# Turning the second part's inputs with VectorE blocks and short DMA runs instead of TensorE transposes, in a long-convolution + gated-MLP kernel

## The chip, the cores and the metric

The kernel runs on one core of one Trainium2 chip. The metric is the device time of the program in microseconds (us); before the change it is 3759.47 us, the median of three runs (3757.68 to 3761.73). The engines are named as in the profile: PE (TensorE matmuls), PEld (TensorE's weight loads, which overlap PE), DVE (VectorE), ACT (ScalarE), POOL (GpSimd) and SP (SyncE, whose queue issues every DMA of this kernel).

## The reference

Everything is float32 in and out.

```python
# first part: x, v are (4, 12480, 128); pos_emb (12480, 64), w1 (64, 64), w2 (64, 128)
h_filt = (np.maximum(pos_emb @ w1, 0.0) @ w2) * np.exp(-0.01 * pos)[:, None]
u = x * v
y = irfft(rfft(u, 2 * S, axis=1) * rfft(h_filt, 2 * S, axis=0))[:, :S, :]   # causal long convolution
z = x * y
# second part: z as (49920, 128); w_in (128, 2048), w_out (2048, 128)
h = z @ w_in
out = (h * np.cos(h)) @ w_out
```

## The kernel before, in words

**First part, the convolution.** Each of the 4 batches is seen as 104 rows (n1, `R`) by 120 columns (n2, `N2`). A forward transform in two stages (`f1`, `f2`), a product with the filter's transform and an inverse transform in two stages (`i1`, `i2`) are all done as matmuls. The last stage, `i2_units`, makes one *group* at a time: 4 values of n2 (`G`), that is 104 rows by 4 x 128 numbers, 30 groups a batch (`NG`), 120 in all. A group is two halves of 4 matmuls (`i2_mm`, L504) with the twiddle table `tm` as weights, and then `i2_out`: VectorE multiplies the PSUM bank by the input x (`xs`) into `zs` (L511), and SP stores the 104 x 512 tile to the DRAM scratch `zd` (L517). While a batch is in `i2`, SP also loads `tm` (312 KB) and `xs` for the next group and, for the next batch, `xt` and `vt`, whose product fills `slots`. In batch 0 most `tm` tables are made on the spot by ACT, DVE and POOL (`make_group`) and stored for the later batches.

**Second part, the MLP.** The 12480 rows of groups (each of 4 tokens) are cut into 98 *blocks* (`NALL`): block 0 is the first group (104 rows), the rest are of 128 rows, the last of 88. A block therefore has up to 512 tokens. Its input must stand with the 128 features on the partitions and the tokens along the free side (`at`). Before the change, `moe_load(n)` (L727) loads 128 rows of `zd` as `zb` (128 x 4 x 128), and `moe_turn(n)` makes four TensorE transposes of 128 x 128 into one PSUM bank (the `transpose` helper, L126) and one ACT copy to `at` (L737). Block 0 skips the DRAM trip: its `zs` is turned directly.

Each block is 16 *steps* (`NFC`). A step is one matmul of 128 x 512 into `ph` (L743), `a` on ACT (L746), the rounding `k` on DVE (L749), the difference `f` on POOL (L752), the sine `cs` on ACT (L757), the product `gt` on DVE (L759), and four steps later (`LAG`) a matmul that adds to `acc` (L768). At the block's end ACT copies `acc` out (L774), four more transposes turn it back, ACT copies them to `ob` (L783) and SP stores it (L794). That is 1568 steps. A 128 x 512 float32 matmul is two passes on TensorE.

**The order of the work.** The program is written in a fixed order (manual schedule), and each engine runs its own instructions in that order. The main loop walks the 1568 steps; after each step it advances the convolution generator `conv` by what the step is owed (`owed`; a unit of `conv` says what it costs in steps). So the first part of batches 1 to 3 runs between the steps of the second part. `load(n)` first advances `conv` until the rows of block n are made. Before the change, `load(n + 2)` is called at step 12 of block n, and `moe_turn(n + 1)` at step 3 of block n. From about 345 us on both parts run together, until the last group at about 2949 us; after that only steps remain.

The SP queue, too, is in order: a DMA whose wait is not met holds all that are behind it. The framework gives DMAs eight completion semaphores in turn, so that a DMA also waits until the one eight places ahead of it has landed.

Tile pools that matter: `zs`, `tm` and `xs` have 2 buffers each in batches 0 to 2 (`tm` and `xs` 3 in the last), `zb` and `at` 2, and the `ph` banks are 4, shared by the steps and the transposes.

Of the kernel before, what the change touches and what calls it, by code (L numbers as in the profile page):

```python
# [9 lines left out]
F32 = mybir.dt.float32  # L10
U32 = mybir.dt.uint32
AF = mybir.ActivationFunctionType
ALU = mybir.AluOpType
# [3 lines left out]
P = 128  # L17
BANK = 512
# [12 lines left out]
def kernel(  # L31
# [46 lines left out]
    nc = tc.nc  # L78

    B, S, D = x.shape  # L80
# [3 lines left out]
    R = S // N2  # L84
# [14 lines left out]
    NFC = DFF // P  # L99
    G = BANK // D  # L100
    UA = 2
    NG = N2 // G
    NROWS = B * NG * R
    NALL = 1 + math.ceil((NROWS - R) / P)
    assert G == 2 * UA and H % UA == 0 and N2 % G == 0
    LAG = 4
    WCOL = 256

    dram = ctx.enter_context(tc.tile_pool(name="dram", bufs=1, space=DRAM))
    hd = dram.tile([N1 // 2, N2, 2, CB, 4], F32, name="hd")  # L110
    zd = dram.tile([NROWS, G, D], F32, name="zd")
    wd = dram.tile([N1 // 2, KE, 2, N2], F32, name="wd")
    td = dram.tile([N2 // G, N1, G, 2, R], F32, name="td")
    wind = dram.tile([D, DFF], F32, name="wind")
# [9 lines left out]
    def transpose(dst, src, ident):  # L124
        n = src.shape[0]
        nc.tensor.transpose(dst, src, ident[0:n, 0:n])  # L126


    def float32_parts(pool, raw):
        lo, hi = raw[:, :, 0], raw[:, :, 1]  # L130

        power = pool.tile([P, WCOL], U32, name="power", bufs=2)
        nc.vector.tensor_scalar(out=power[:, :], in0=hi, scalar1=20, scalar2=0x7FF,
# [5 lines left out]

        sig = pool.tile([P, WCOL], U32, name="sig", bufs=2)  # L140
        nc.vector.tensor_scalar(out=sig[:, :], in0=hi, scalar1=0xFFFFF, scalar2=0x100000,
                                op0=ALU.bitwise_and, op1=ALU.bitwise_or)
        high = sig[:, :].bitcast(F32)
        nc.scalar.activation(high, sig[:, :], AF.Copy, scale=2.0 ** -20)
        low = pool.tile([P, WCOL], F32, name="low", bufs=1)
        nc.scalar.activation(low[:, :], lo, AF.Copy, scale=2.0 ** -52)
# [3 lines left out]
    def float32_join(dst, raw, power, high):  # L150
# [6 lines left out]
        if dst.space == DRAM:  # L157
# [3 lines left out]
    out_words = moe_w_out.bitcast(U32).rearrange("(c p) (q w) -> p c q w", p=P, w=2)  # L161
    in_pieces = [(slice(c, c + WCOL), in_words[:, c:c + WCOL, :])
                 for c in range(0, DFF, WCOL)]
    out_pieces = [(slice(c, c + WCOL // D), out_words[:, c:c + WCOL // D, :, :])
                  for c in range(0, NFC, WCOL // D)]
# [110 lines left out]
    def last_tables(pool):  # L276
        rows = pool.tile([N1, 4, R], F32, name="rows")

        tw_t = pool.tile([N1, 2, N2], F32, name="tw_t")
        return rows, tw_t  # L280
# [226 lines left out]
    def i2_out(pool, ps, xs, b, g):  # L507
        if b == 0:
            yield
        zs = pool.tile([R, 2, UA, D], F32, name="zs")  # L510
        nc.vector.tensor_tensor(  # L511
            zs[:, :, :, :].rearrange("p h n d -> p (h n d)"), ps[0:R, :],
            xs[:, :, :].rearrange("p h n -> p (h n)"), op=ALU.mult)
        z = zs[:, :, :, :].rearrange("p h n d -> p (h n) d")
        row = (b * NG + g) * R
        if row > 0:
            nc.sync.dma_start(zd[row:row + R, :, :], z)  # L517
        else:
            zbs[0] = z
        made[0] += 1  # L520
        yield

    rows_psum = []
    made = [0]
    zbs = {}

# [187 lines left out]
    ats, accs = {}, {}  # L716

    def first_row(n):
        return min(R + (n - 1) * P, NROWS) if n else 0

    def rows_of(n):
        return first_row(n + 1) - first_row(n)

    def moe_load(pool, n):
        m, row = rows_of(n), first_row(n)
        zb = pool.tile([P, G, D], F32, name="zb", bufs=2)
        nc.sync.dma_start(zb[0:m, :, :], zd[row:row + m, :, :])  # L727
        zbs[n] = zb

    def moe_turn(pool, n):  # L730
        m = rows_of(n)
        zb = zbs.pop(n)
        pt = ps_h.tile([P, BANK], F32, name="ph")
        for i in range(G):
            transpose(pt[:, i * m:(i + 1) * m], zb[0:m, i, :], ident)
        at = pool.tile([D, BANK], F32, name="at")
        nc.scalar.copy(out=at[:, 0:G * m], in_=pt[:, 0:G * m])  # L737
        ats[n] = at

    def moe_up(pool, n, c):  # L740
        m = G * rows_of(n)
        ph = ps_h.tile([P, BANK], F32, name="ph")
        nc.tensor.matmul(ph[:, 0:m], w_in_sb[:, c * P:(c + 1) * P], ats[n][:, 0:m],  # L743
                         start=True, stop=True)
        a = pool.tile([P, BANK], F32, name="a", bufs=3)
        nc.scalar.activation(a[:, 0:m], ph[:, 0:m], AF.Identity,  # L746
                             bias=quarter[:, 0:1], scale=INV_TWO_PI)
        k = pool.tile([P, BANK], F32, name="k")
        nc.vector.tensor_scalar(out=k[:, 0:m], in0=a[:, 0:m], scalar1=ROUND,  # L749
                                scalar2=ROUND, op0=ALU.add, op1=ALU.subtract)  # L750
        f = pool.tile([P, BANK], F32, name="f")
        nc.gpsimd.tensor_tensor(f[:, 0:m], a[:, 0:m], k[:, 0:m], op=ALU.subtract)  # L752
        return ph, f, m

    def moe_act(pool, ph, f, m):
        cs = pool.tile([P, BANK], F32, name="cs")
        nc.scalar.activation(cs[:, 0:m], f[:, 0:m], AF.Sin, scale=TWO_PI)  # L757
        gt = pool.tile([P, BANK], F32, name="gt", bufs=4)
        nc.vector.tensor_tensor(gt[:, 0:m], ph[:, 0:m], cs[:, 0:m], op=ALU.mult)  # L759
        return gt  # L760

    def moe_down(n, c, gt):
        if c == 0:

            accs[n] = bank() if made[0] == B * NG and n % 2 else \
                ps_acc.tile([P, BANK], F32, name="acc")
        m = G * rows_of(n)
        nc.tensor.matmul(accs[n][:, 0:m], w_out_sb[:, c, :], gt[:, 0:m],  # L768
                         start=(c == 0), stop=(c == NFC - 1))

    def moe_evict(pool, n):
        m = G * rows_of(n)
        ot = pool.tile([D, BANK], F32, name="ot", bufs=1)
        nc.scalar.copy(out=ot[:, 0:m], in_=accs.pop(n)[:, 0:m])  # L774
        return ot

    def moe_back(pool, n, ot):
        m = rows_of(n)
        pt = ps_h.tile([P, BANK], F32, name="ph")
        for i in range(G):  # L780
            transpose(pt[0:m, i * D:(i + 1) * D], ot[:, i * m:(i + 1) * m], ident)
        ob = pool.tile([P, 2, UA * D], F32, name="ob", bufs=1)
        nc.scalar.copy(out=ob[0:m, :, :].rearrange("p h n -> p (h n)"), in_=pt[0:m, :])  # L783
        return ob
# [15 lines left out]
    with tc.manual_schedule():  # L800
        with tc.tile_pool(name="psum", bufs=8, space=PSUM) as psum, \
                ExitStack() as first:
            def bank():
                return psum.tile([P, BANK], F32, name="ps")
# [11 lines left out]
            with tc.tile_pool(name="layers", bufs=1, side="right") as pool:  # L816
# [14 lines left out]
                ident = pool.tile([P, P], F32, name="ident")  # L831
# [65 lines left out]
            rows, tw_t = last_tables(wpool)  # L897
            for kept, here in ((rowsd, rows), (twd, tw_t)):
                nc.sync.dma_start(here[:, :, :], kept[:, :, :])
            ident = wpool.tile([P, P], F32, name="ident")  # L900
# [17 lines left out]
        nc.scalar.copy(out=table, in_=rows[:, :, :])  # L918
        rows_psum.append(table)
        mpool = ctx.enter_context(tc.tile_pool(name="moe", bufs=2))  # L920

        def bank():
            return ps_c[0].tile([P, BANK], F32, name="cv")
# [15 lines left out]
        def load(n):  # L939
            while made[0] * R < first_row(n + 1):  # L940
                next(conv)
            moe_load(mpool, n)

        while made[0] == 0:
            next(conv)
        moe_turn(mpool, 0)
        steps = [(n, c) for n in range(NALL) for c in range(NFC)]
        hidden, gates, ots, obs = {}, {}, {}, {}
        for i in range(len(steps) + LAG):
            if i < len(steps):  # L950
                n, c = steps[i]
                if n == 0 and c == NFC // 2:
                    load(1)
                if c == NFC - 4 and n + 2 < NALL:
                    load(n + 2)
                hidden[i] = moe_up(mpool, n, c)
            if i >= LAG:
                pn, pc = steps[i - LAG]
                moe_down(pn, pc, gates.pop(i - LAG))
                if pc == NFC - 1:  # L960
                    ots[pn] = moe_evict(mpool, pn)
            if 0 <= i - 1 < len(steps):
                gates[i - 1] = moe_act(mpool, *hidden.pop(i - 1))
            if i < len(steps):

                if c == (LAG - 1 if n else NFC - 2) and n + 1 < NALL:
                    moe_turn(mpool, n + 1)
                if c == NFC // 2 and n - 1 in ots:
                    obs[n - 1] = moe_back(mpool, n - 1, ots.pop(n - 1))
                if c == NFC // 2 + 2 and n - 1 in obs:  # L970
                    moe_store(n - 1, obs.pop(n - 1))
            owed += 1.0
            while owed > 0.0:
                owed -= next(conv, owed)
# [30 lines left out]
```

## Time and profile before

| | |
|---|---|
| device time, median of 3 runs | 3759.47 us (3757.68 to 3761.73) |
| the profiled execution, first to last instruction | 3758.9 us, TensorE clock granted 0.995 |
| busy: PE / DVE / ACT / POOL | 98% / 74% / 67% / 68% |
| DMA queue of SP | 209,239 packets, 273.12 MB, 24.8% of the 16 engines' span |
| transposes of `zb` (L126) | 388, in 97 blocks |
| ACT copies to `at` (L737) | 98 |
| `zs` products on DVE (L511) | 120, mean 680 ns |

In the profile, PE's busy time overlaps its neighbours': a pass of a 128 x 512 matmul shows about 0.59 us, while the next pass starts some 0.43 us after it. The stages are best told apart by time: up to about 340 us the filter and the first forward transforms; 345 to 575 us `i2` of batch 0; 600 to 1170 us the transforms of batch 1, 1170 to 1390 us its `i2`; the same again to about 1995 and 2215 us; then batch 3, with its `i2` from about 2800 to 2949 us; then steps alone. The profile page gives no time of the profiled execution other than its span.

### The profile page before, as it was taken

How to read it: one execution, taken by the hardware profiler on the slowest of the kernel's cores; microseconds unless marked ns; L12 is line 12 of the kernel's file. 1: busy time of each engine (PE TensorE's matmuls, PEld its weight loads, DVE VectorE, ACT ScalarE, POOL GpSimd, SP SyncE). 2: the span in 40 equal slices, each digit the busy share in tenths (PEclk: the TensorE clock that was granted, in tenths of full speed). 3: DMA queues.
4: the chain of work that ended last, by engine and by line, in shares of the span. 5: the costliest groups of instructions: out<-in, count | busy, mean ns of one | idle time of the engine just before them, and what ended most of it. 6: DMA issues, size and time to landing. Idle time of an engine off the chain costs nothing.

```text
span 3758.9 us, 47177 instructions
## 1 busy us (share of the span) xinstructions
PE 3690.6 (98%) x13546; PEld 2110.4 (56%) x13546; DVE 2773.7 (74%) x5586; ACT 2508.2 (67%) x4660; POOL 2557.6 (68%) x2318
## 2 busy tenths in 40 slices
PE   7898999999999999999999999999999999999999
PEld 6777555555566556555565556555566544444444
DVE  8887997687866787788766776788765666666666
ACT  5757776766665557766665567666664677777777
POOL 6666776588845665688745664788644677777776
PEclk9999999999999999999999999999999999999999
DMA  6263551022203650122104530122105200000000
GB/s 167 64 185 107 155 167 33 25 72 79 72 12 91 181 151 12 40 79 77 52 18 128 180 105 21 52 79 76 38 21 172 76 23 17 17 23 18 17 23 13
DMA packets 209499, 276.14 MB, mean 73 GB/s; under 512 B 17111, under 2 KB 146535, under 8 KB 209111
## 3 DMA queue, kind: packets, MB, share of 16 engines
q1 hardware_dynamic: 209239, 273.12, 24.8%
q8 instruction: 109, 1.79, 0.2%
q14 instruction: 151, 1.24, 0.1%
HBM read 193.64 MB, written 79.42 MB: 73 GB/s over the span
## 4 chain that ended last, share of the span: by engine, by line
PE 88%; DVE 3%; POOL 3%; ACT 2%; DMA 2%; issue 1%; SPq 0%; POOLq 0%; DVEq 0%; ACTq 0%
PE ph L743 33%; PE acc L768 28%; PE cv L504 5%; PE cv L768 5%; PE cv L479 4%; PE cv L407 3%; PE cv L448 3%; PE ph L126 2%; POOL f L752 1%; PE ps L407 1%; PE ps L448 1%; DMA tm<-td 1%; DMA wd<-w 1%; ACT cs L757 1%; DVE k L749 1%
## 5 line engine op out<-in xcount | busy, mean ns | idle before, releaser
L752 POOL TENSOR_TENSOR f<-a,k 128x512 f32<-128x512 f32 (+1 forms) x1568 | 1986.2, 1267 | 1060.5 <-DVE k L749 1059.1
L743 PE MATMUL ph<-at,w_in_sb 128*128 128x512 f32 (+1 forms) x3136 | 1599.0, 591 | 3.7 <-DVE gt L759 2.7
L746 ACT ACTIVATE a<-ph,quarter 128x512 f32<-128x512 f32 (+1 forms) x1568 | 1071.2, 683 | 704.8 <-PE ph L743 695.2
L768 PE MATMUL acc<-gt,w_out_sb 128*128 128x512 f32 (+1 forms) x2688 | 1370.3, 591 | 0.0
L759 DVE TENSOR_TENSOR gt<-ph,cs 128x512 f32<-128x512 f32 (+1 forms) x1568 | 1077.3, 687 | 359.9 <-ACT cs L757 341.8
L757 ACT ACTIVATE cs<-f 128x512 f32<-128x512 f32 (+1 forms) x1568 | 981.0, 626 | 366.6 <-POOL f L752 364.3
L749 DVE TENSOR_SCALAR k<-a 128x512 f32<-128x512 f32 (+1 forms) x1568 | 792.9, 506 | 550.7 <-ACT a L746 524.2
L768 PEld LDWEIGHTS acc<-gt,w_out_sb 128*128 128x128 f32 x2688 | 508.4, 189 | 642.8 <-issue 631.9
L743 PEld LDWEIGHTS ph<-at,w_in_sb 128*128 128x128 f32 x3136 | 553.2, 190 | 337.7 <-issue 257.5
L474 POOL TENSOR_TENSOR slots<-slots,t 120x256 f32<-120x256 f32 x384 | 312.9, 821 | 59.9 <-DVE t L467 25.6
L504 PEld LDWEIGHTS cv<-slots,tm 96*104 96x104 f32 x1920 | 238.6, 169 | 106.8 <-issue 85.4
L504 PE MATMUL cv<-slots,tm 96*104 96x128 f32 x1920 | 251.7, 273 | 9.9 <-POOL tm L297 5.0
L768 PE MATMUL cv<-gt,w_out_sb 128*128 128x512 f32 (+1 forms) x448 | 224.5, 583 | 1.0 <-DVE gt L759 1.0
L479 PEld LDWEIGHTS cv<-cs,slots 120*96 120x96 f32 x1536 | 176.7, 167 | 67.2 <-issue 65.2
L479 PE MATMUL cv<-cs,slots 120*96 120x120 f32 x1536 | 183.2, 266 | 0.0
L448 PEld LDWEIGHTS cv<-slots,w 124*120 124x120 f32 x576 | 103.7, 184 | 124.3 <-issue 112.3
L407 PEld LDWEIGHTS cv<-c,slots 104*124 104x124 f32 x768 | 132.6, 192 | 72.2 <-issue 60.0
L448 PE MATMUL cv<-slots,w 124*120 124x256 f32 x576 | 173.0, 380 | 0.0
L407 PE MATMUL cv<-c,slots 104*124 104x192 f32 x768 | 151.8, 327 | 5.4 <-DVE gt L759 3.5
L768 PEld LDWEIGHTS cv<-gt,w_out_sb 128*128 128x128 f32 x448 | 84.9, 190 | 104.8 <-issue 99.5
L489 DVE TENSOR_TENSOR slots<-cv,other 96x240 f32<-96x240 f32 x384 | 133.1, 394 | 1.5 <-ACT other L487 1.4
L395 DVE TENSOR_TENSOR xt<-xt,vt 104x256 f32<-104x256 f32 x177 | 132.6, 751 | 0.6 <-DMA vt<-in_v_dram 0.6
(131 smaller groups left out, 2520.9 us busy)
## 6 DMA issues: line engine op xcount, KB each, us to landing
h<-hd SPq DMA_DIRECT2D x144, 240.0 KB
tm<-td SPq DMA_DIRECT2D x96, 312.0 KB
xt<-in_x_dram SPq DMA_DIRECT2D x120, 208.0 KB
vt<-in_v_dram SPq DMA_DIRECT2D x120, 208.0 KB
xs<-in_x_dram SPq DMA_DIRECT2D x120, 208.0 KB
zd<-zs SPq DMA_DIRECT2D x119, 208.0 KB
zb<-zd SPq DMA_DIRECT2D x96, 256.0 KB
w<-wd SPq DMA_DIRECT2D x144, 116.2 KB
```

The lines of the kernel that those rows point to most:

```text
L407: nc.tensor.matmul(ps[0:KE, i * 2 * N1:(i + 1) * 2 * N1], u[:, b, 0:KE, i], c1[0:u.shape[0], :, :].rearrange("p r k -> p (r k)"), start=Tr ...
L448: nc.tensor.matmul(pi, w[:, i, :], parts[0:KE, :, k], start=True, stop=True)
L474: nc.gpsimd.tensor_tensor(y[:, r], y[:, r], t[:, r], op=op)
L479: nc.tensor.matmul(ps[0:N1, (i * 2 + r) * N2:(i * 2 + r + 1) * N2], parts[0:N2, r, :, b, i], cs[:, r, :], start=True, stop=True)
L504: nc.tensor.matmul(ps[0:R, i * D:(i + 1) * D], t[:, i, r, :], slots[0:N1, :, place, :], start=(r == 0), stop=(r == 1))
L743: nc.tensor.matmul(ph[:, 0:m], w_in_sb[:, c * P:(c + 1) * P], ats[n][:, 0:m], start=True, stop=True)
L746: nc.scalar.activation(a[:, 0:m], ph[:, 0:m], AF.Identity, bias=quarter[:, 0:1], scale=INV_TWO_PI)
L749: nc.vector.tensor_scalar(out=k[:, 0:m], in0=a[:, 0:m], scalar1=ROUND, scalar2=ROUND, op0=ALU.add, op1=ALU.subtract)
L752: nc.gpsimd.tensor_tensor(f[:, 0:m], a[:, 0:m], k[:, 0:m], op=ALU.subtract)
L757: nc.scalar.activation(cs[:, 0:m], f[:, 0:m], AF.Sin, scale=TWO_PI)
L759: nc.vector.tensor_tensor(gt[:, 0:m], ph[:, 0:m], cs[:, 0:m], op=ALU.mult)
L768: nc.tensor.matmul(accs[n][:, 0:m], w_out_sb[:, c, :], gt[:, 0:m], start=(c == 0), stop=(c == NFC - 1))
```

## The change

`zs` becomes two fixed tiles of 128 partitions (`zss`; partitions 96 to 127 are cleared once by GpSimd, so that the rows above 104 are defined), used in turn. After the product, DVE transposes the tile in blocks of 32 x 32 into a new tile `zt`, reading features with a stride of 4, and SP stores all 128 partitions of `zt` to `zd`, whose layout is now by group: in each quarter of 32 rows, feature d of the four n2 stands as 4 runs of 32 tokens. `moe_load` now loads straight into `at`: for each piece of rows that lies in one quarter of one group there is one DMA of 128 partitions x 4 runs of up to 32 tokens (128 bytes), 5 to 7 DMAs for a block of 128 rows, 542 in all for blocks 1 to 97. `moe_turn` and its copies go; block 0 keeps its TensorE transposes. `load(n + 1)` is now called at step 2 of block n, six steps later for the same block than before; `load(1)` stays at step 8 of block 0.

```diff
-    zd = dram.tile([NROWS, G, D], F32, name="zd")
+    zd = dram.tile([B * NG, P, BANK], F32, name="zd")
...
     def i2_out(pool, ps, xs, b, g):
         if b == 0:
             yield
-        zs = pool.tile([R, 2, UA, D], F32, name="zs")
-        nc.vector.tensor_tensor(
-            zs[:, :, :, :].rearrange("p h n d -> p (h n d)"), ps[0:R, :],
-            xs[:, :, :].rearrange("p h n -> p (h n)"), op=ALU.mult)
-        z = zs[:, :, :, :].rearrange("p h n d -> p (h n) d")
-        row = (b * NG + g) * R
-        if row > 0:
-            nc.sync.dma_start(zd[row:row + R, :, :], z)
-        else:
-            zbs[0] = z
+        zs = zss[made[0] % 2]
+        nc.vector.tensor_tensor(zs[0:R, :], ps[0:R, :],
+                                xs[:, :, :].rearrange("p h n -> p (h n)"), op=ALU.mult)
         made[0] += 1
+        if made[0] == 1:
+            return
+        zt = pool.tile([P, BANK], F32, name="zt")
+        nc.vector.transpose(zt[:, :].rearrange("p (j n a) -> p j n a", j=D // SQ, n=G),
+                            zs[:, :].rearrange("p (n a j) -> p j n a", n=G, j=D // SQ))
+        nc.sync.dma_start(zd[b * NG + g, :, :], zt[:, :])
         yield
...
     def moe_load(pool, n):
         m, row = rows_of(n), first_row(n)
-        zb = pool.tile([P, G, D], F32, name="zb", bufs=2)
-        nc.sync.dma_start(zb[0:m, :, :], zd[row:row + m, :, :])
-        zbs[n] = zb
-
-    def moe_turn(pool, n):
-        m = rows_of(n)
-        zb = zbs.pop(n)
+        at = pool.tile([D, BANK], F32, name="at")
+        to = at[:, 0:G * m].rearrange("d (i n) -> d i n", i=G)
+        done = 0
+        while done < m:
+            group, n1 = divmod(row + done, R)
+            rows = min(m - done, R - n1, SQ - n1 % SQ)
+            there = zd[group, n1 // SQ * SQ:n1 // SQ * SQ + SQ, :]
+            nc.sync.dma_start(
+                to[:, :, done:done + rows],
+                bass.AP(tensor=there.tensor, offset=there.offset + n1 % SQ,
+                        ap=[[G * SQ, D], [SQ, G], [1, rows]]))
+            done += rows
+        ats[n] = at
+
+    def moe_turn_first(pool):
         pt = ps_h.tile([P, BANK], F32, name="ph")
         for i in range(G):
-            transpose(pt[:, i * m:(i + 1) * m], zb[0:m, i, :], ident)
+            transpose(pt[:, i * R:(i + 1) * R], zss[0][0:R, i * D:(i + 1) * D], ident)
         at = pool.tile([D, BANK], F32, name="at")
-        nc.scalar.copy(out=at[:, 0:G * m], in_=pt[:, 0:G * m])
-        ats[n] = at
+        nc.scalar.copy(out=at[:, 0:G * R], in_=pt[:, 0:G * R])
+        ats[0] = at
...
+        zss = [mpool.tile([P, BANK], F32, name=f"zs{i}", bufs=1) for i in range(2)]
+        for zs in zss:
+            nc.gpsimd.memset(zs[R // SQ * SQ:P, :], 0.0)
...
                 if n == 0 and c == NFC // 2:
                     load(1)
-                if c == NFC - 4 and n + 2 < NALL:
-                    load(n + 2)
+                if c == 2 and 0 < n < NALL - 1:
+                    load(n + 1)
...
-                if c == (LAG - 1 if n else NFC - 2) and n + 1 < NALL:
-                    moe_turn(mpool, n + 1)
```

More of the change, by code (lines that the diff above doesn't have):

```diff
@@ L106 @@
     LAG = 4
+    SQ = 32
     WCOL = 256
@@ L524 @@
     made = [0]
-    zbs = {}
     def units(n, steps, before, mm, after, parts, ahead=2, skip=0):
@@ L945 @@
             next(conv)
-        moe_turn(mpool, 0)
+        moe_turn_first(mpool)
         steps = [(n, c) for n in range(NALL) for c in range(NFC)]
```

## The prediction

> **What bounds the kernel now.** I read the busy shares first, then PE's timeline in the last third, then the busy times of three stages, and last the SP queue of one `i2` stage, where the new loads will stand.
>
> ```profile
> PE 3690.6 (98%) x13546; PEld 2110.4 (56%) x13546; DVE 2773.7 (74%) x5586; ACT 2508.2 (67%) x4660; POOL 2557.6 (68%) x2318
> ```
>
> PE is the bound, by a share that allows about 70 us of idle time. What a transpose costs it is seen in the timeline of PE alone (start, us, operation):
>
> ```profile
> 3308.72 1.02 PE L743 MATMUL ph<-at,w_in_sb 128*128 128x512 f32 x2
> 3309.58 1.02 PE L768 MATMUL cv<-gt,w_out_sb 128*128 128x512 f32 x2
> 3310.44 0.60 PE L126 MATMUL ph<-ident,zb 128*128 128x128 f32 x4
> 3310.88 1.02 PE L743 MATMUL ph<-at,w_in_sb 128*128 128x512 f32 x2
> 3311.74 1.02 PE L768 MATMUL acc<-gt,w_out_sb 128*128 128x512 f32 x2
> ```
>
> The matmuls start 0.86 us apart without a hole, and the four transposes of a block put 0.44 us between two of them. Read so for all 97 blocks, from the first transpose to the next matmul, the median is 0.437 us and the sum 43.6 us. The other engines by stage (`i2` of batches 0, 1 and 2, then the steps alone):
>
> ```profile
> 345.00:575.00 230.00, 227.66 (x912) 131.08 (x911) 211.56 (x369) 169.92 (x334) 177.84 (x165) 1.00 0.52 158
> 1170.00:1380.00 210.00, 208.35 (x877) 122.58 (x876) 159.62 (x286) 116.78 (x192) 132.01 (x113) 1.00 0.58 173
> 2000.00:2210.00 210.00, 207.16 (x851) 119.83 (x850) 160.15 (x285) 116.45 (x190) 133.87 (x114) 1.00 0.58 174
> 2960.00:3740.00 780.00, 780.00 (x1988) 357.39 (x1987) 503.57 (x885) 607.72 (x967) 559.96 (x443) 1.00 0.07 18
> ```
>
> The columns are the span, the busy time of PE, PEld, DVE, ACT and POOL, the granted clock, the DMA engines' share and GB/s. In batch 0 DVE is busy 211.6 of 230 us: 18.4 us are left in the only stage where it is as full as PE. In batches 1 and 2 it has 50 us left each. The DMA engines are over half busy in every `i2` stage and nearly idle at the end. The SP queue in batch 1:
>
> ```profile
> 1272.42 0.31 SPq L376 DMA_DIRECT2D xs<-in_x_dram  x1
> 1272.83 0.35 SPq L676 DMA_DIRECT2D tm<-td  x1
> 1273.22 0.38 SPq L517 DMA_DIRECT2D zd<-zs  x1
> 1273.71 0.33 SPq L376 DMA_DIRECT2D xt<-in_x_dram  x1
> 1277.25 0.33 SPq L376 DMA_DIRECT2D vt<-in_v_dram  x1
> 1279.79 0.31 SPq L376 DMA_DIRECT2D xs<-in_x_dram  x1
> ```
>
> Between `vt` and the next `xs` SP waits some 2.1 us, for a buffer. The last packet of a `tm` load lands 3.0 to 3.5 us after its issue, and the group that reads it starts 5.1 us after the issue: `tm` has 1.6 to 2 us to spare and is the tightest transfer of the kernel.
>
> **The change part by part.**
>
> *Removed from PE:* 97 turns, 43.6 us. 7 of them lie in 345 to 575 us, where DVE will decide; I count their 3.1 us as no gain there. That leaves -40.5 us. *Removed from ACT:* 97 copies of 0.574 us, 56 us; ACT is 78% busy at most in the stages above and ends no chain of note, so nothing, unless the shorter ACT queue helps batch 0. *Removed from SP:* 97 loads of 0.39 us. *Freed:* one use in 17 of a `ph` bank; PE has no holes that it could close in the steps alone.
>
> *Added to DVE:* 119 transposes of 128 x 512. No row shows one. From below: the quickest SBUF-to-SBUF instruction of this size, `k`, takes 0.41 us undisturbed. From above: two plain copies of that size; a PSUM copy of 64 x 384 takes 0.539 us, so one of 512 is estimated at 0.67 (384 elements and 512 elements at 1.04 ns, with 0.14 fixed), two at 1.34. I take 0.67, since a block transpose reads and writes each element once as a copy does; the next instruction starts 0.08 us before the end of the one before (the 0.68 us `zs` products), and the new wait for `zs` on the same engine gives about that back. Behind the waiting transpose stand `gt` and `k` of the steps, and for `gt` waits PE.
>
> - Batch 0: 29 x 0.67 = 19.4 us into 18.4 us of idle time. If all of it could be filled, +1; if none, +19. Two engines that are both full do not fill each other's holes, and the waits here are short (`gt` and `k` waited 15 us in all). I take half: +10. With 0.41 us the ends are 0 and 12, with 1.34 us 20 and 39.
> - Batches 1 and 2: 60 x 0.67 = 40 us into 100 us. In 600 to 1000 us DVE was 77% busy and PE had no hole; here it goes from 76% to 86%. +3, between 0 and 8.
> - Batch 3: 30 into 70 us free, 53% to 67% busy: nothing; the cover is the idle DVE, and without it 20 us at most.
>
> *Moved and multiplied:* each block's one load becomes 5 to 7 DMAs, 542 for 97, of 512 packets of at most 128 bytes, and comes six steps later, at step 2 of the block before. It is needed 14 steps later: 14 x 1.72 = 24 us in the steps alone, more beside the convolution. The price of one in the SP queue: 16 packets took 0.28 us to issue, 208 took 0.33, 480 (`pe`) 0.48 when nothing was in the way. So about 0.5, and 5.6 of them 2.8 us. In the DMA engines: packets of 256 bytes took 15 to 18 ns, of 512 bytes 25 to 27, of 4 bytes 9; for 128 bytes I estimate 13 ns, x 32 packets an engine = 0.42 us; the upper end is `pe`, ten DMAs of 480 packets of four times the size, issued in 8.33 us when the engines were full: about 1.0 us landed each. A block then costs 2.8 to 6 us, landed within 9 at the most. It is in time by 15 us.
>
> What queues behind the burst matters more. In the order of the changed program the burst stands after `vt` and before `xs` and `tm`, five times in batch 1 and five in batch 2. SP's 2.1 us of waiting hide most of 2.8 us: `tm` is issued 0.7 to 1.2 us later, within its slack of 1.6 to 2. At 1.0 us each the DMA engines hold it 3.5 us, 2 beyond the slack. So 0 to 20 us for ten bursts; I take 0.5 each, +5, because 13 ns is nearer to the 256-byte row than to the full queue. In `f2` the loads of `w` and `h` are two periods of 5.8 us ahead: 3 us of burst is hidden; that cover is gone if a burst exceeds some 6 us. In batch 3 `tm` has a third buffer. The `zb` loads, which delayed `tm` in a few periods of batches 1 and 2 (PE stood 3.2 us for `tm` in batch 1), go; I count nothing.
>
> *Other edits with one answer:* the store of `zt` waits for the transpose, 0.7 us later, with `xt` behind it, whose buffers are three; it moves 128 rows for 104 and leaves the engines as it found them. Two memsets on POOL, some 0.5 us each by the row of the 104 x 512 memset (527 ns), hold the first `zs` by 1 us at most. Following the loop, block 24's load no longer pulls three units of `conv` ahead (4.5 steps), so the convolution ends five steps later; PE does the same work.
>
> The pages of the Trainium skill speak both ways. "VectorE: DVE Perf Modes", section "The three transpose paths", gives 311 ns for a 128 x 128 block on VectorE in two-byte type and 390 on TensorE, and its rule table advises TensorE for 128 x 128. Four such blocks would be 1.24 us by that page, an estimate; by the copy row 0.67. With the page's price the sum would be: batch 0 +20, batches 1 and 2 +10, in all -5 instead of -22. The same section warns that a plain DMA which transposes by strides is 19 times slower than the crossbar path (1309 ns); four blocks would then take an estimated 100 us, more than a block's 27.5 us, and the loads would bound everything. Here the innermost run is contiguous, which the warning does not cover, and no run so far shows it.
>
> **Sum.** -40.5 + 10 + 3 + 5 = -22.5 us from a profiled span of 3758.9 gives 3736.4. The median of the runs is 0.6 us above that span, so 3737.0 us.
>
> **The rivals.**
>
> *Nothing is paid.* DVE fills its idle time and the bursts hide: -43.6 to -40.5, 3716 to 3719 us. For it: ACT is relieved in batch 0, and 0.41 us would fit. Against: DVE there has only gaps of about 0.4 us.
>
> *The short runs hold `tm` (ends slower).* If one DMA takes 2 us in the engines, a burst is 11 us; less 2.1 of SP's idle time and 1.8 of slack, PE stands 7 us in each of ten bursts: 70 - 27.5 = +43, 3802 us; with `f2` behind it too (some 35 blocks at 5 us) far more. It decides from 1.3 us a DMA, or 40 ns a packet: 5.6 x 1.3 = 7.3, a stall of 3.4, x 10 = 34. For it: the trace has no loads of 128-byte packets. Against: the 256- and 512-byte rows.
>
> *The transpose takes two passes, 1.34 us.* Batch 0 pays 20 to 39 us, batches 1 and 2 go to 95% of DVE and pay 5 to 10 each: -40.5 + 30 + 15 + 5 = +10, 3769 us.
>
> *The turn's time does not come back:* the freed matmul slots wait for a late `at` at each block's start. At 15 us of reserve this needs a burst of 20 us; 3760 us or more.
>
> **How the numbers follow.** A measurement of this kernel can tell about 0.2%, 7.5 us: faster is below 3752, slower above 3767. The forecast case, 3722 to 3752: 0.60. Nothing paid: 0.12. Two-pass transposes, 3750 to 3785: 0.12, split over the three. `tm` held mildly, 3745 to 3767: 0.08; held beyond, and the late `at`: 0.08 in all. Faster: 0.60 + 0.12 + 0.02 = 0.74; same 0.11; slower 0.15. The range runs from the first rival, 3715, to the middle of the two-pass case, 3770.
>
> **What would show it.** Right: no L126 rows with `zb`, about 119 DVE transposes of 0.6 to 0.7 us, PE's matmuls 0.86 us apart through the whole end, DVE above 95% from 345 us on and that stage some 10 us longer. Wrong: DMA `tm<-td` or `at<-zd` as a releaser of PE with more than 10 us; a transpose over 1 us; SP issues of `at` over 0.8 us. The prediction fails first if a 128-byte packet costs 40 ns or more.

## The result, and the profile after

The changed kernel takes 3774.06 us (median of five runs, 3769.41 to 3777.28) beside 3759.47 us for the kernel before in the same runs. The ratio is 1.0036, with a 95% interval of 1.0025 to 1.0047. It is 14.6 us slower; the forecast was 22.5 us faster. The time lies just outside the range of 3715 to 3770 us.

The profiled execution took 3769.41 us, with a span of 3767.6 us at a granted clock of 0.993. It is 4.7 us below the kernel's median, so a comparison of the two profiles understates the loss by about that much. The busy shares:

```profile
PE 3667.9 (97%) x13158; PEld 2066.9 (55%) x13158; DVE 2903.8 (77%) x5705; ACT 2448.9 (65%) x4563; POOL 2548.6 (68%) x2320
```

PE has 388 instructions fewer and VectorE 130 us more. In the steps alone the change does just what was forecast. PE's timeline in the last third (start, us, operation):

```profile
3308.26 1.02 PE L753 MATMUL ph<-at,w_in_sb 128*128 128x512 f32 x2
3309.12 1.02 PE L778 MATMUL cv<-gt,w_out_sb 128*128 128x512 f32 x2
3309.98 1.02 PE L753 MATMUL ph<-at,w_in_sb 128*128 128x512 f32 x2
3310.84 1.02 PE L778 MATMUL cv<-gt,w_out_sb 128*128 128x512 f32 x2
3311.70 1.02 PE L753 MATMUL ph<-at,w_in_sb 128*128 128x512 f32 x2
```

The matmuls start 0.86 us apart and the 0.44 us of the turn between two of them is gone. The busy times by stage, in the same windows and columns as before (span; PE, PEld, DVE, ACT, POOL; clock, DMA share, GB/s), show where it is lost again:

```profile
345.00:575.00 230.00, 216.19 (x840) 122.09 (x840) 212.53 (x370) 155.19 (x309) 165.38 (x155) 0.99 0.54 156
1170.00:1380.00 210.00, 203.60 (x837) 116.11 (x836) 182.13 (x305) 116.21 (x191) 123.25 (x107) 1.00 0.54 157
2000.00:2210.00 210.00, 204.44 (x828) 116.14 (x827) 181.29 (x300) 114.57 (x188) 122.59 (x107) 0.99 0.56 160
2960.00:3740.00 780.00, 779.89 (x1941) 353.93 (x1940) 511.58 (x897) 600.24 (x942) 563.04 (x444) 1.00 0.12 22
```

PE's idle time in these windows grows from 2.3 to 13.8 us in batch 0, from 1.7 to 6.4 in batch 1 and from 2.8 to 5.6 in batch 2. At the end it stays at nothing. VectorE is no fuller in batch 0 than it was (212.5 of 230 us, 211.6 before), where the forecast looked for over 95%: the added work did not go into its idle time, the stage grew longer. What PE waited for, before (engine, operation, releaser: us in all, times, longest):

```profile
PE cv L504 <- DMA tm<-td: 4.8, 6, 1.4
PE ph L743 <- DVE gt L759: 2.7, 5, 0.8
```

and after:

```profile
PE cv L505 <- DMA tm<-td: 16.3, 19, 1.8
PE ph L753 <- DVE gt L769: 12.6, 19, 2.6
PE acc L778 <- ACT ot L784: 9.1, 10, 2.1
```

Three waits take 30 us more: for the table `tm`, for `gt` behind VectorE's queue, and for ACT's copy of `acc`, for which PE has no row before. The added instruction itself, by tile (count, then shortest, median and longest in ns, first and last start in us):

```profile
L518 DVE STREAM_TRANSPOSE zt<-zs x119: 1091/1119/1199, 353.7 to 2978.6; 128x512 f32<-128x512 f32 x119
```

It takes 1.12 us, not 0.67: 133 us of VectorE in all, where 80 were booked. VectorE's timeline in batch 0 shows one of them:

```profile
426.86 0.69 DVE L769 TENSOR_TENSOR gt<-ph,cs 128x512 f32<-128x512 f32 x1
427.47 0.68 DVE L512 TENSOR_TENSOR zs<-cv,xs 104x512 f32<-104x512 f32 x1
428.19 1.15 DVE L518 STREAM_TRANSPOSE zt<-zs 128x512 f32<-128x512 f32 x1
429.22 0.42 DVE L396 TENSOR_TENSOR xt<-xt,vt 104x256 f32<-104x256 f32 x1
429.52 0.45 DVE L759 TENSOR_SCALAR k<-a 128x512 f32<-128x512 f32 x1
429.86 0.72 DVE L769 TENSOR_TENSOR gt<-ph,cs 128x512 f32<-128x512 f32 x1
```

There is no gap on VectorE, and from one `gt` to the next pass 3.0 us. On PE an up matmul and a down matmul take 1.72 us.

To compare stages over kernels I read PE's holes from the starts of its matmuls: the time from one start to the next, less 0.837 ns for each column, which is what a pass takes when nothing holds it (512 columns in 0.429 us, the median before). Summed over the program, PE's work falls from 3620.7 to 3579.3 us (-41.4) and its holes grow from 129.9 to 179.4 us (+49.5). By stage, in us (e1 to e11 are the runs below):

| stage (us) | before | after | e1 no transposes | e3 also no short loads | e11 also GpSimd relieved | e5b plain columns |
|---|---|---|---|---|---|---|
| `i2` of batch 0 (340 to 620) | 13.0 | 32.0 | 21.0 | 18.8 | 18.3 | 30.2 |
| `i2` of batch 1 (1165 to 1440) | 7.5 | 17.0 | 8.2 | 6.1 | 6.1 | 10.0 |
| `i2` of batch 2 (1995 to 2285) | 8.8 | 20.3 | 9.1 | 8.2 | 10.4 | 10.1 |
| the three transforms between (620 to 1165, 1440 to 1995, 2285 to 2800) | 14.2 | 23.9 | 21.6 | 21.7 | 13.0 | 22.2 |
| start, batch 3 and end | 86.5 | 86.1 | 86.0 | 85.7 | 86.0 | 86.4 |
| all | 129.9 | 179.4 | 145.9 | 140.5 | 133.8 | 158.8 |

Batches 0 to 2 lose 40 us of the 49.5, and the transforms between them, where no VectorE transpose runs at all, lose 10. How far one profile can be trusted: e7 and e12, whose `i2` stages of batches 0 to 2 are nearly those of the kernel before, have holes of 15.7, 8.3 and 8.7 us and of 13.2, 7.0 and 8.1 us there, so a difference of less than some 3 us in one stage says nothing.

### The profile page after: what moved, and what is told of

Its sections match the earlier page's. It is cut to its first block, busy times and chain, and to the rows that moved or that the text cites. A ratio compares the mean times of both kernels' runs of the same rounds, so it can differ in the third digit from the quotient of the medians.

```text
span 3767.6 us, 47271 instructions
## 1 busy us (share of the span) xinstructions
PE 3667.9 (97%) x13158; PEld 2066.9 (55%) x13158; DVE 2903.8 (77%) x5705; ACT 2448.9 (65%) x4563; POOL 2548.6 (68%) x2320
## 4 chain that ended last, share of the span: by engine, by line
PE 80%; POOL 6%; DVE 5%; ACT 3%; DMA 3%; issue 3%; SPq 0%; DVEq 0%; POOLq 0%; ACTq 0%
PE ph L753 30%; PE acc L778 25%; PE cv L778 5%; PE cv L505 5%; PE cv L480 4%; POOL f L762 4%; PE cv L408 3%; PE cv L449 3%; DMA tm<-td 2%; ACT cs L767 1%; DVE k L759 1%; PE ps L449 1%; DVE gt L769 1%; PE ps L408 1%; PE ph L127 1%
## 5 line engine op out<-in xcount | busy, mean ns | idle before, releaser
L759 DVE TENSOR_SCALAR k<-a 128x512 f32<-128x512 f32 (+1 forms) x1568 | 824.3, 526 | 416.3 <-ACT a L756 392.6
L505 PE MATMUL cv<-slots,tm 96*104 96x128 f32 x1920 | 255.4, 275 | 21.8 <-DMA tm<-td 16.3
L518 DVE STREAM_TRANSPOSE zt<-zs 128x512 f32<-128x512 f32 x119 | 133.4, 1121 | 4.1
```

Of the source, the lines that this page charges most:

```text
L505: nc.tensor.matmul(ps[0:R, i * D:(i + 1) * D], t[:, i, r, :], slots[0:N1, :, place, :], start=(r == 0), stop=(r == 1))
```

## The experiments

Four reasons stood against each other: the transposes fill VectorE; the bursts of short loads hold `tm`; the turn had covered a wait on PE that is now bare; and something other than PE sets the pace of a stage, so that its time there was not PE's to give. Times are given as the difference to the kernel before in the same runs.

**e1: no transpose.** The tile is stored as it is.

```diff
-        zt = pool.tile([P, BANK], F32, name="zt")
-        nc.vector.transpose(zt[:, :].rearrange("p (j n a) -> p j n a", j=D // SQ, n=G),
-                            zs[:, :].rearrange("p (n a j) -> p j n a", n=G, j=D // SQ))
-        nc.sync.dma_start(zd[b * NG + g, :, :], zt[:, :])
+        nc.sync.dma_start(zd[b * NG + g, :, :], zs[:, :])
```

> The product tile is stored to DRAM untransposed (the output is then not the reference's); the short loads and their place stay. Theory D (the 1.12 us transposes fill DVE in the i2 stages of batches 0 to 2, and PE waits for gt): PE's idle time in those three stages falls from 69 us to 35 or less, and the time from 3774 to 3735-3745. Theory L (the bursts of short loads hold tm): it falls by less than 8 us, to 3766 or more, and PE still waits some 16 us for tm.

Measured: 3733.48 us, -27.4; ratio 0.9924 [0.9908, 0.9941].

**e2: one load a block.** The 5 to 7 short loads of a block become one load of whole rows.

```diff
-        to = at[:, 0:G * m].rearrange("d (i n) -> d i n", i=G)
-        done = 0
-        while done < m:
...
-            done += rows
+        nc.sync.dma_start(at[:, 0:G * m], zd[(row + m - 1) // R, :, 0:G * m])
```

> Each block's 5 to 7 short-run loads become one load of 128 rows of up to 2 KB (wrong data, so the output is not the reference's); the transposes stay. Theory D: 3760 to 3768, since only the waits of PE for tm go (16 us of releaser time, of which the kernel before also had 5). Theory L: 3740 or less.

Measured: 3769.58 us, +8.7; ratio 1.0023 [1.0014, 1.0032].

**e3: neither.** Both edits together.

> Neither the transposes nor the short loads (the output is not the reference's). If D and L are all there is, the whole 41 us of PE's freed time shows: 3716 to 3722. Theory A (the four transposes on PE also covered the wait of the next block's first acc matmul for ACT's copy of the last acc, L784, which is now exposed): 10 us or so stay, 3727 to 3735, with ACT ot L784 still among PE's releasers.

Measured: 3731.19 us, -29.7; ratio 0.9920 [0.9905, 0.9935].

e1 came out 1.5 us below and e2 1.6 us above the range of theory D, and both far from theory L; e3 lies in the range of theory A, which e6 tests.

What follows from the three: the transposes cost 42.0 us with the short loads in place (+14.6 to -27.4) and 38.4 without them (+8.7 to -29.7). The short loads cost 5.9 us with the transposes and 2.3 without. The intervals of these ratios reach 3 to 6 us to either side, so the price of the transposes is clear of them and that of the loads hardly is. PE's wait for `tm`, 16.3 us after, is 4.0 in e1 and 9.5 in e2, so it was mostly the transposes that made `tm` late; by which path (the store of `zt` ahead of the next loads on SP, or a group's bank released late) these runs do not show. The burst itself, on SP in batch 1 of the changed kernel:

```profile
1201.34 0.34 SPq L675 DMA_DIRECT2D tm<-td  x1
1202.09 0.35 SPq L520 DMA_DIRECT2D zd<-zt  x1
1202.53 5.22 SPq L735 DMA_DIRECT2D at<-zd  x5
1207.86 0.53 SPq L377 DMA_DIRECT2D xs<-in_x_dram  x1
1208.51 0.32 SPq L675 DMA_DIRECT2D tm<-td  x1
```

Five loads hold the queue 5.2 us here, 1.0 us each, the upper end of the forecast; over the program's 543 short loads the median is 0.63 us. In the DMA engines a packet of 128 bytes took 13 ns (median of 148,480), as estimated. And with both costs out of the way, only 29.7 of the 41.4 us that left PE were saved. e6 and e9 to e12 look for the rest.

**e4: the reordering, moved.** VectorE's product reads plain columns and writes the features in the order that the transpose wants, so that neighbouring features land 128 columns apart; the transpose reads and writes plain columns.

```diff
+        if made[0] > 0:
+            dst = dst.rearrange("p (j n a) -> p n a j", j=D // SQ, n=G)
+            src, xin = (t.rearrange("p (n a j) -> p n a j", n=G, j=D // SQ)
+                        for t in (src, xin))
+        nc.vector.tensor_tensor(dst, src, xin, op=ALU.mult)
...
-        nc.vector.transpose(zt[:, :].rearrange("p (j n a) -> p j n a", j=D // SQ, n=G),
-                            zs[:, :].rearrange("p (n a j) -> p j n a", n=G, j=D // SQ))
+        nc.vector.transpose(zt[:, :], zs[:, :])
```

> The stride of 4 moves from the transpose's reads to the product's writes; the transpose reads and writes 512 contiguous columns, and the result is the same. If the stride made the transpose slow: it falls from 1.12 to about 0.67 us, the product stays near 0.68, and the time falls to 3750-3760. If float32 transposes take two passes whatever the stride: 1.1 us still, and 3770-3778.

Measured: 3773.94 us, +13.0; ratio 1.0034 [1.0021, 1.0047]. The tile's rows in this kernel:

```profile
L517 DVE TENSOR_TENSOR zs<-cv,xs x120: 691/1059/1091, 342.3 to 2982.7; 104x512 f32<-104x512 f32 x120
L522 DVE STREAM_TRANSPOSE zt<-zs x119: 710/711/715, 354.5 to 2983.7; 128x512 f32<-128x512 f32 x119
```

The transpose falls to 0.71 us, and the product rises from 0.68 to 1.06 us, where the theory that blamed the stride expected it to stay near 0.68. The reordering costs some 0.4 us in whichever of the two instructions does it, as reads four columns apart or as writes 128 columns apart, and the kernel's time stays where it was.

**e5: no stride at all.** The product as in the changed kernel, the transpose on plain columns (features then stand in another order).

> The transpose reads and writes its 512 columns as they stand (the features then lie in another order, so the output is not the reference's); everything else is as in the changed kernel, the product too. The transpose should take 0.71 us, as in e4, for 1.12. If the loss goes with DVE's time (40 us for 1.12 us each): 25 us are left of it, 3757 to 3761. If it starts where DVE is full (18 us of idle time in batch 0): more goes, 3745 to 3753. If the transposes cost by what they hold up whatever their length: 3768 or more.

Measured: 3748.05 us, -14.2; ratio 0.9960 [0.9946, 0.9973].

**e5b: no stride, and the reference's output.** Features are grouped by 32 neighbours instead of by every fourth, so that the transpose moves plain runs; to put each feature's 128 tokens together, every quarter of 32 partitions is stored by a DMA of its own in runs of 512 bytes.

```diff
-        nc.vector.transpose(zt[:, :].rearrange("p (j n a) -> p j n a", j=D // SQ, n=G),
-                            zs[:, :].rearrange("p (n a j) -> p j n a", n=G, j=D // SQ))
-        nc.sync.dma_start(zd[b * NG + g, :, :], zt[:, :])
+        nc.vector.transpose(zt[:, :].rearrange("p (j n c) -> p n j c", j=D // SQ, n=G),
+                            zs[:, :].rearrange("p (n j c) -> p n j c", n=G, j=D // SQ))
+        for q in range(P // SQ):
+            there = zd[b * NG + g, q * SQ:(q + 1) * SQ, :]
+            nc.sync.dma_start(
+                bass.AP(tensor=there.tensor, offset=there.offset,
+                        ap=[[G * SQ, SQ], [SQ * G * SQ, D // SQ], [1, G * SQ]]),
+                zt[q * SQ:(q + 1) * SQ, :].rearrange("p (j k) -> p j k", j=D // SQ))
```

> The same short transpose with the right result: the features are split as j, a, and each quarter of 32 partitions is stored by a DMA of its own in runs of 512 bytes, so that the loads stay as they are. Three stores more a group, some 0.4 us each in the SP queue and 512 packets for 128. If the stores are hidden: as e5_plain_columns, within 3 us. If they hold tm and xs further: 5 us or more above it, with more waits of PE for tm.

Measured: 3748.19 us, -14.1; ratio 0.9961 [0.9947, 0.9974]. It beats both kernels. Its transpose, by tile:

```profile
L518 DVE STREAM_TRANSPOSE zt<-zs x119: 711/711/714, 352.9 to 2958.0; 128x512 f32<-128x512 f32 x119
```

Its output too is in another order than its input, but in runs of 32 columns, and it takes no longer than e5's: what costs is the step between neighbouring reads. So 0.41 us less on each of 119 transposes (49 us of VectorE) is worth 28.7 us of time, while the first 0.71 us of each (85 us of VectorE) costs only 13.3 us (e1 to e5b). The price per microsecond of VectorE rises from 0.16 to 0.59.

**e6: the kernel before with its turn nine steps later.** It asks whether the turn's place covered a wait.

```diff
-                if c == (LAG - 1 if n else NFC - 2) and n + 1 < NALL:
+                if c == (NFC - 4 if n else NFC - 2) and n + 1 < NALL:
```

> The kernel before, with the four transposes on PE moved from step 3 of a block to step 12; nothing is added or removed. Theory A (at step 3 they cover the wait of the next acc matmul for ACT's copy L774): ACT ot becomes a releaser of PEld and PE with some 25 us (5 before), PE's holes at step 4 grow by 5 to 10 us, and the time rises to 3764-3772. If the place does not matter: 3757 to 3762.

Measured: 3758.41 us, -3.9; ratio 0.9995 [0.9976, 1.0015]. The turn's place does not matter, and PE's wait for ACT's `ot` copy, which it might have covered at step 3, is 0.7 us with the turn gone from there. That reason falls for the kernel before. (The ratio takes in one run of 3799 us; the other ten took 3755 to 3760.)

**e7: VectorE turns for batch 3 only.** Batches 0 to 2 keep TensorE's turns (24 turns go, for the blocks from 74 on); the transpose is the changed kernel's 1.12 us one. (e7 and e8 have one `zs` tile for it, where the changed kernel has two, and one `zb` buffer, where the kernel before has two.)

```diff
+    DB = 3
+    N0 = 1 + math.ceil((DB * NG * R - R) / P)
...
+        if b >= DB:
+            zt = pool.tile([P, BANK], F32, name="zt")
...
-                if c == (LAG - 1 if n else NFC - 2) and n + 1 < NALL:
+                if c == (LAG - 1 if n else NFC - 2) and n + 1 < N0:
```

> The kernel before for the rows of batches 0 to 2; only the groups of batch 3 are turned by DVE and loaded in short runs (blocks 74 to 97). There DVE is 53% busy and the changed kernel had no more holes in PE than the one before. 24 turns of 0.437 us go, 10.5 us: 3749 to 3752. If the loads or the transposes hold something at the end too: 3757 or more.

Measured: 3751.32 us, -11.0; ratio 0.9969 [0.9956, 0.9981]. Where VectorE has room and only steps follow, the 24 x 0.437 = 10.5 us come back, within an interval of some 5 us.

**e8: VectorE turns from batch 1 on,** with e5b's transpose and stores (`DB = 1` in the diff above). **e9: the end of a block in another bank.** In e5b, the four transposes that turn a block's result back use, from batch 1 on, one of the convolution's three PSUM banks. **e10: both.**

```diff
-        pt = ps_h.tile([P, BANK], F32, name="ph")
+        if ps_c[0] is two_banks:
+            pt = ps_h.tile([P, BANK], F32, name="ph")
+        else:
+            pt = ps_c[0].tile([P, BANK], F32, name="cv")
```

> Batch 0 turns its blocks on TensorE as before; from batch 1 on VectorE transposes plain runs of 32 columns (0.71 us) and four stores write each tile. If batch 0 is where VectorE has no room and the other three have it: 73 turns of 0.437 us go, 32 us, and some 3 us more of holes in i2 of batches 1 and 2 and 7 us in the transforms between come back, so 3737 to 3746 us beside 3760 before. If the 0.71 us hurts i2 of batches 1 and 2 as much as batch 0, 3746 to 3752, like the kernel with four stores in every batch.

> The kernel with four stores in every batch (3748.2), and from batch 1 on the four transposes at a block's end write to one of the convolution's three PSUM banks instead of one of the steps' four. Theory that the steps lack a bank after step 8: the hole of some 6 us in all at step 9 of the transform stages falls to about 1 and nothing comes in its place, 3741 to 3744 us. Theory that TensorE, rid of the turns, runs up against the pace of the chain of ACT, GpSimd and VectorE behind a step: the hole moves to other steps or to the convolution's banks, 3746 to 3750 us.

> Both of the other two edits: TensorE turns in batch 0, VectorE from batch 1 on, and the end of a block in a convolution bank. If the two losses are separate: 4 to 6 us below the kernel that has the first edit alone, 3732 to 3741 us; if the pace of the chain decides, the same time as that kernel within 2 us.

Measured: e8 3749.13 us, -11.9, ratio 0.9965 [0.9951, 0.9978]; e9 3764.00 us, +3.0, ratio 1.0004 [0.9996, 1.0013]; e10 3761.01 us, 0.0, ratio 0.9998 [0.9989, 1.0006]. e9 and e10 missed both of their ranges, and e9 is 17 us slower than e5b, on which it is built. e8 missed the range of the theory that only batch 0 is short of VectorE; it lies in the other's, but not by that theory's reason. In e8 the holes of batch 0 are back at 13.5 us, but its 24 turns are back on PE too, and `i2` of batches 1 and 2 has 15.0 and 14.4 us of holes instead of 10.0 and 10.1. PE's row for `tm` in e8:

```profile
PE cv L508 <- DMA tm<-td: 15.2, 14, 2.1
```

Four stores a group hold SP 1.9 us; why they hurt `tm` more here than in e5b (8.9 us) was not found. e9 did not free PE: the holes at step 9 of the blocks fell from 6.6 to 1.8 us in the transforms, and those at step 8 grew from 1.3 to 17.3 us, where the convolution's matmuls now waited for their bank. The convolution's three banks have none to spare, and these stages lost time in both arrangements, which pointed to an engine behind the banks.

**e11 and e12: GpSimd relieved in `f2`.** In the transforms, GpSimd does two jobs: `f` of each step, and the sums of `f2`'s product. By group, in 760 to 1000 us of the kernel before (busy us, mean ns | idle before, and for what):

```profile
L752 POOL TENSOR_TENSOR f<-a,k 128x512 f32<-128x512 f32 x116 | 147.8, 1274 | 23.6 <-DVE k L749 23.6
L474 POOL TENSOR_TENSOR slots<-slots,t 120x256 f32<-120x256 f32 x80 | 68.0, 850 | 5.7 <-DVE t L473 3.8 <-PE acc L768 0.5 <-PE cv L448 0.2
```

A step's `f` and one sum are 2.12 us on GpSimd. On PE the two matmuls of a step and the two short passes of `f2` beside it are 2.16 us (two neighbouring `acc` matmuls start at 851.47 and 853.63 us). GpSimd's idle time of 29.3 us in the window is 0.15 us for each of 196 instructions: in this stage it is the fullest engine after PE. e11 is e3, and e12 the kernel before, with the sums on half of their columns:

```diff
-            nc.gpsimd.tensor_tensor(y[:, r], y[:, r], t[:, r], op=op)
+            part = CB if whole else CB // 2
+            nc.gpsimd.tensor_tensor(y[:, r, 0:part], y[:, r, 0:part], t[:, r, 0:part], op=op)
```

> The kernel without transposes and without short loads, and in f2 of the batches that run beside the second part GpSimd's sum works on half of its columns (0.85 us to about 0.45, about 40 us of GpSimd in each of three f2 stages; the output is not the reference's). Theory that GpSimd paces f2 (in 760 to 1000 us it did 196 instructions before and 197 without any transposes, so the steps came no faster): the 8 blocks of each f2 give back their 0.44 us each, 3 x 3.5 us = 10 us, so 3719 to 3726 us, and the holes from 620 to 1165 us fall from 7.3 to below 4 us. Theory that VectorE, a bank or the order of waits holds f2: 3728 to 3733 us.

> The same edit of GpSimd's sums in the kernel before (output not the reference's). There TensorE has no holes in f2 (720.0 of 720 us busy in three windows), so both theories expect no gain worth the name: 3755 to 3761 us. If GpSimd already held the kernel before in f2, 3745 to 3752 us, and then the gain in the kernel without transposes says nothing of the turn.

Measured: e11 3719.97 us, -40.8, ratio 0.9891 [0.9876, 0.9906]; e12 3759.06 us, -1.7, ratio 0.9995 [0.9987, 1.0004]. The same window in the kernel before:

```profile
760.00:1000.00 240.00, 240.00 (x680) 122.12 (x679) 194.92 (x391) 160.08 (x254) 210.69 (x196) 1.00 0.26 77
```

in e3:

```profile
760.00:1000.00 240.00, 239.22 (x657) 120.21 (x656) 202.25 (x392) 153.75 (x248) 211.27 (x197) 1.00 0.27 78
```

and in e11:

```profile
760.00:1000.00 240.00, 240.00 (x664) 121.17 (x663) 183.55 (x397) 155.39 (x250) 191.71 (x198) 1.00 0.27 79
```

Without the turns PE issues 23 instructions fewer in the 240 us of e3 and the other engines do hardly more: the stage goes on at its old pace. What the steps wait for is seen on ACT, whose sine `cs` takes GpSimd's `f`; its row in the same window (busy us, mean ns | idle before, and for what), before, in e3 and in e11:

```profile
L757 ACT ACTIVATE cs<-f 128x512 f32<-128x512 f32 x116 | 73.0, 629 | 36.1 <-POOL f L752 35.8
L754 ACT ACTIVATE cs<-f 128x512 f32<-128x512 f32 x116 | 73.2, 631 | 75.4 <-POOL f L749 75.3
L755 ACT ACTIVATE cs<-f 128x512 f32<-128x512 f32 x118 | 73.9, 626 | 5.4 <-POOL f L750 5.3
```

Without the turns ACT waits 75 us for GpSimd instead of 36, and with shorter sums 5. With GpSimd relieved PE is full again, and its holes in the three transforms fall from 21.7 to 13.0 us, below those of the kernel before (14.2). The hole at step 9 of the blocks, where an up matmul comes late, falls from 6.3 us to 0.8. PE's wait for ACT's `ot` copy is still 4.3 us (6.2 in e3), so it is not what e11 won back. GpSimd's sums withheld the 11.1 us between e3 and e11 (some 8 us more or less by the two intervals; 6.9 by the spans of the two profiles); in the kernel before the same relief brings 1.7, within its interval. Both lie in the ranges of the theory that GpSimd paces `f2`, though the holes from 620 to 1165 us fall to 4.3 us and not below 4. Two limits of this reading. GpSimd is not full in e3 either (211 of 240 us): that a lag is not caught up at 2.12 us a step beside 2.16 is the likely way, and no run shows it by itself. And VectorE's busy time falls too, from 202 to 184 us at about the same count of instructions. It is the rounding `k` alone that gets shorter, from a mean of 692 ns in e3 (598 before) to 432; `gt` and the two products of `f2` keep theirs. So the runs show that GpSimd's sums hold the stage back, and not how much of it by their own length and how much by slowing `k` beside them.

## Why the prediction was wrong, by its own steps

*Removed from PE, -40.5 us.* Right as work: PE's matmul time falls by 41.4 us, and with transposes, short loads and GpSimd's sums out of the way the kernel is 40.8 us faster. The rival "nothing is paid" was put at 3716 to 3719 us; e11 took 3720, though with less work on GpSimd. What was wrong is that only batch 0 was counted as a stage where PE's time isn't PE's to give. The transforms were taken as PE's because it had no hole there; GpSimd was nearly as full and went unpriced. That omission is worth some 7 to 11 us (29.7 us saved in e3 instead of 40.8 by the medians, 6.9 by the profiles).

*Added to DVE, 119 transposes at 0.67 us: +10 in batch 0, +3 in batches 1 and 2.* This is the step that failed, and the term was mis-sized: they take 1.12 us and cost 38 to 42 us in time. The argument that a block transpose reads and writes each element once, as a copy does, held for plain columns: 0.71 us, and e5b against e1 gives 13.3 us for them, where the forecast had 13. By stage the holes grow by 9.2 us in batch 0 and 2.8 in batches 1 and 2, where it had 10 and 3; so close a match is partly luck, since the two intervals allow some 8 us either way. It did not hold for the access pattern in the diff, which reads every fourth feature; the stride was described in the text and not priced. The page "VectorE: DVE Perf Modes" of the Trainium skill, section "The three transpose paths", gives 311 ns for a two-byte 128 x 128 block. Four of them made the estimate of 1.24 us, which the prediction passed over for the copy row. For the kernel as changed it was the nearer of the two; for plain columns it was not.

*Where it would be paid.* Batch 0 was named as the tightest stage and is: +19.0 us of holes, against +13.1 in the forecast's terms (10, and the 3.1 not counted as a gain). Batches 1 and 2 were taken as nearly covered, since VectorE was left idle time there; they lose 9.5 and 11.5 us against 3 and 5 for both. VectorE's 50 us of idle time in 1170 to 1380 us before came in 109 pieces, half of them of 0.41 us or less, and pieces of over 1.1 us make up 6 us of it; they did not hold an instruction of 1.1 us that the steps' `gt` queues behind. With 0.71 us their holes return to 10.0 and 10.1. Batch 3 and the steps alone were booked at nothing, and that was right (holes 6.8 before, 7.0 after; e7 gains its full 11.0).

*Load bursts, +5 us.* The measured 2.3 to 5.9 us agree with it as far as the intervals go. The issue was 0.63 us by the median, and 1.0 in the burst shown, which is over the 0.8 that was named as a sign of being wrong; the packets took the estimated 13 ns. The rival of 3802 us fell with it. The page's warning of a 19-fold slower DMA, in the same section, is for a large innermost stride; the runs of this kernel are contiguous.

*ACT relief, nothing; the other edits, nothing.* The store of `zt`, which waits for the transpose with the next loads behind it, was booked at nothing, and `tm` was feared for the bursts alone. But PE's wait for `tm`, 16.3 us, falls to 8.9 in e5b and to 4.0 without the transpose, with the short loads in place in both: a part of the transposes' price came by `tm` and not by `gt`. No run shows a gain from ACT's shorter queue. PE's wait for ACT's `ot` copy rose to 9.1 us, is 6.2 in e3 and 4.3 in e11, and is not explained one by one.

*The rivals.* "Two passes, 1.34 us" with 3769 us came closest to the 3774, with a chance of 0.12. Its threshold was right (a transpose over 1 us spoils the change) and its reason was not: on plain columns the transpose takes 0.71 us, and e4 shows that the reordering costs about as much in a product as in a transpose. The late `at` did not occur. Two counts in the prediction were off without weight: there are 543 short loads, not 542, and the turn was one use of a `ph` bank in 18 (16 steps, the turn and the block's end), not in 17.

Summed anew: -41.4, +42.0 for transposes at 1.12 us, +2.3 for the loads, +11.1 for `f2` is +14.0 us, beside 14.6 measured. The last three terms are differences between the runs themselves, so this sum tests no more than that e11 saves what left PE. Some 5 us of holes in batch 0 remain in e11 (18.3 against 13.0 before) and were not taken apart.

## What to carry to other kernels

Price an instruction with the access pattern it will have: the same transpose cost 0.71 us on plain columns and 1.12 us with reads four columns apart, and that difference alone turned a gain of 14 us into a loss of 14. Before work is taken from the bounding engine, look stage by stage for a second engine whose period is nearly the same (here GpSimd's 2.12 us against PE's 2.16), because there the freed time can stay with the other engine. An engine's idle share is no cover for an instruction longer than its gaps, when the bounding engine waits for what queues behind it.

## What the runs showed of the hardware that was not expected

A step between neighbouring float32 columns cost VectorE about 0.4 us on 512 columns: 4 columns in the reads of a transpose (0.71 to 1.12 us), 128 columns in the writes of a product (0.68 to 1.06 us). Halving GpSimd's sums in the kernel before (from a mean of 850 ns to 586, 80 of them in 760 to 1000 us) also took VectorE from 194.9 to 182.5 us busy in that window, at 391 and 392 instructions; the mean of `k` fell from 598 to 435 ns and the others kept theirs. PE's time did not move there, so in that kernel neither was worth anything.
